# Q, K and V of the last two chunks as pairs of 64-row matmuls inside the gate-up stages

## The chip, the cores and the metric

The kernel runs on one core of one Trainium2 chip. The metric is device time in microseconds (us) of one execution, lower is better. The core's engines run side by side: TensorE (PE, with its weight loads PEld), VectorE (DVE), ScalarE (ACT), GpSimd (POOL) and SyncE (SP). SP and POOL issue nearly all DMAs here.

## The reference

One transformer block with modulation over S = 2048 tokens of D = 576 values, all bf16:

```
sa, ca, ga, sb, cb, gb = silu(c) @ w_mod            # six rows of 576
h = layernorm(x) * (1 + ca) + sa
q, k, v = h @ wqkv                                  # 32 heads of 18
attention: each token sees itself and the tokens 2, 4, .. 14 before it (8 logits, softmax)
x = x + ga * (attention @ wo)
h = layernorm(x) * (1 + cb) + sb
x = x + gb * (((h @ w_gate) * (h @ w_up)) @ w_down)  # width 4608
```

576 is four and a half times 128. A matmul that contracts over all 128 rows of the array needs five passes over 576, the last of them half empty. Two matmuls of 64 rows each can stand side by side in the array; 576 is nine times 64.

## The kernel before

**Chunks and groups.** Attention (the A part) works on eight chunks of 256 tokens. The feed-forward part works on five groups of 128-token tiles, `GROUPS = [(0, 2), (2, 6), (6, 10), (10, 13), (13, 16)]`: group 0 is chunk 0, group 1 chunks 1 and 2, group 2 chunks 3 and 4, group 3 chunk 5 and half of 6, group 4 the rest. Each group has a gate-up stage (`gate_up`, L651) and a down stage (`down`, L713). They alternate: gate-up 0, down 0, gate-up 1, down 1 and so on. The order of instructions on every engine is the order in which the program emits them (`manual_schedule`), and each engine works through its own in order.

**Gate-up.** It runs over 36 column tiles `f` of the width 4608. For each, the gate result goes to PSUM bank `pg` and the up result to `pu`. All its matmuls are 64 rows high and come in pairs: the lower half of the array works for one bank, the upper half for the other. `first_part` does five pairs (the 64 left-over rows, which `wgr` and `h2T` hold for both, then four), `second_part` does four pairs with the banks swapped. A wait (`swap`) stands ahead of the second part, so that both halves never write the same bank. The second part of tile f comes after the first part of tile f+1. Then ACT copies `pu` and `pg` to `u_sb` and `g_sb` (L683, L684), and DVE multiplies them into `hh` (L688). PSUM has eight banks, one pool (`ps`) for everything.

**Background of the gate-up stages.** Attention from the products of Q and K on: `b_p` (L424, DVE), logits `b_lq` (L434), softmax, weighting of shifted values and sums. `values(i)` issues `b_ld`, which loads the shifted values `vsh` of chunk i from a DRAM buffer `vd`. `B_two` orders two chunks, `B_one` one chunk. Each piece has a cost, and `spread` lays the list evenly over the column tiles.

**Down.** It runs over the 36 row tiles of w_down. Each of the group's token tiles gets a 512-column matmul into `acc` (L726) and a 64-column one into `accr` (L730). Its background, spread one piece after another over the first 32 steps, is made by `out_qkv(i, n)`: for chunk i the output projection (`b_o`, `b_w` L577), the second layer norm (`b_ln`, `b_norm`) and the transposes `b_t` that make `h2T`; and for chunk n the first layer norm (`a_ln`, `a_norm`), the transposes `a_t` that make `hT`, then five pieces `a_q` (L376) and two pieces `a_v` (L399, L401). A piece `a_q` does two column tiles of Q or of K with five 128-row matmuls each; the middle one does the left-over 64 columns of Q and of K together (`wq4`). ACT copies the results to `qT` and `kT`, and `a_halo` copies 16 earlier keys. `a_v` does one row tile of V as 504 and 72 columns; ACT copies to `v_sb`, and POOL stores that to `vd`. The rows 64 to 127 of the fifth row tile of `wqk`, `wv` and of the modulation columns `modc` are zero.

**Where chunks 5 to 8 stand.** Down 1 has `out_qkv(3, 5) + out_qkv(4, 6)` (32 pieces), down 2 has `out_qkv(5, 7) + out_qkv(6, 8)` (24 pieces; there is no chunk 8). The attention of chunk 6 is in gate-up 2, that of chunk 7 in gate-up 3.

**Weights.** `load_wgu` (L150, SP) and `load_wd` (L165, POOL) stream the gate, up and down weights in blocks of four tiles, into three buffers each.

Of the kernel before, what the change touches and what calls it, by code (L numbers as in the profile page):

```python
# [7 lines left out]
BF = mybir.dt.bfloat16  # L8
F32 = mybir.dt.float32
# [29 lines left out]

MODK = (0, 4, 1, 2, 3)  # L40
QKK = (0, 1, 4, 2, 3)
GROUPS = [(0, 2), (2, 6), (6, 10), (10, 13), (13, 16)]


@with_exitstack
def kernel(
# [47 lines left out]
    def js(j):  # L94
        return slice(j * P, (j + 1) * P)
# [5 lines left out]
    ind = consts.tile([P, KT, H], BF, name="ind")  # L101
    addc = consts.tile([P, 2, KT], F32, name="addc")
    eps = consts.tile([P, 1], F32, name="eps")
    modc = consts.tile([P, 4, KT], F32, name="modc")
    ga_bc = consts.tile([P, D], BF, name="ga_bc")
    gb_bc = consts.tile([P, D], BF, name="gb_bc")
    sc = consts.tile([P, KT], BF, name="sc")
# [175 lines left out]
    def modulate(dst, s, m, vi_scale, vi_shift, on_dve):  # L283
        if on_dve:
            nc.vector.tensor_scalar(dst, s, modc[:, vi_scale, m:m + 1], modc[:, vi_shift, m:m + 1], ALU.mult, ALU.add)  # L285
        else:
            nc.scalar.activation(dst, s, ACTF.Identity, bias=modc[:, vi_shift, m:m + 1], scale=modc[:, vi_scale, m:m + 1])

    def transposed(src, dst, cols, vi, between=None):
        n = P * len(cols)  # L290
        pA = ps([P, 3, n], BF, "tr_pA")
        pB = ps([P, 2, n], BF, "tr_pB")
        for c, j in enumerate(cols):
            if c and between:
                between()
            for m in range(KT):
                d = pA[:, m, :] if m < 3 else pB[:, m - 3, :]
                nc.tensor.transpose(d[:, js(c)], src[:, j, m * P:(m + 1) * P], ident[:])  # L298

        def evict(on_dve=(0, 1, 2)):  # L300
            for m in range(KT):
                s = pA[:, m, :] if m < 3 else pB[:, m - 3, :]
                modulate(dst(m), s, m, vi + 1, vi, m in on_dve)
        return evict

    def mod_columns(wm, pi):
# [50 lines left out]
    def a_t(i, on_dve=(0, 1, 2), between=None):  # L357
        a_tiles(i)
        hT = aa[i]["hT"]
        transposed(aa[i]["xn"], lambda m: hT[:, m, :], (0, 1), 0, between)(on_dve)  # L360

    def qk_w(kt, m):
        if m == KF:
# [30 lines left out]
    def a_v(i, j):  # L394
        hT = aa[i]["hT"]
        pv = ps([P, VA * DH], F32, "pv")
        pvr = ps([P, VR * DH], F32, "pvr")
        for kt in range(KT):
            nc.tensor.matmul(pv[:], lhsT=hT[:, kt, js(j)], rhs=wv[:, kt, 0:VA * DH], start=(kt == 0), stop=(kt == KT - 1))  # L399
        for kt in range(KT):  # L400
            nc.tensor.matmul(pvr[:], lhsT=hT[:, kt, js(j)], rhs=wv[:, kt, VA * DH:D], start=(kt == 0), stop=(kt == KT - 1))  # L401
# [95 lines left out]
    def b_o(i):  # L497
# [120 lines left out]
    def B_one(a, av_a):  # L618
        return B_pr(a, 0, 6) + B_lq(a, 0) + B_pr(a, 6, 8) + B_wait(1.5) + B_lq(a, 1) + B_wait(4.0) + B_sm(a) + av_a

    def B_av(i):
        r = []
# [6 lines left out]

    def out_qkv(i, n):  # L630
        o = [lambda: b_o(i), lambda: b_w(i, 0), lambda: b_w(i, 1), lambda: b_ln(i), lambda: b_norm(i), lambda: b_t(i, (0,) if i == 6 else (0, 1))]
        if n >= NCH:
            return [o[0], nop, o[1], o[2], o[3], o[4], nop, o[5]]
        q, v = [lambda g=g: a_q(n, g) for g in range(5)], [lambda j=j: a_v(n, j) for j in range(ST)]
        return ([lambda: a_ln(n), o[0], lambda: (a_norm(n), load_x(n + 2))] + [nop] * (3 if n == 4 else 0) + [o[1], lambda: a_t(n), o[2], o[3]] + q[:1] + [o[4]] + q[1:]
                + [o[5]] + v)
# [14 lines left out]
    def gate_up(gi, hh, bg):  # L651
        N = P * (GROUPS[gi][1] - GROUPS[gi][0])
        ht = h2T[gi]
        at = spread(bg, FT)
        lo, hi = slice(0, 64), slice(64, P)
        pgu = {}

        def half(bank, lhs, rhs, first, last):
            return nc.tensor.matmul(bank[:, 0:N], lhsT=lhs, rhs=rhs, start=first, stop=last, skip_group_check=True)  # L659

        def first_part(f):
            wb = wgu_blk[gi * NBLK + f // FB]
            cs = slice((f % FB) * P, (f % FB + 1) * P)
            pg, pu = ps([P, 2 * CH], F32, "pg"), ps([P, 2 * CH], F32, "pu")
            half(pg, wgr[lo, js(f)], ht[lo, KF, 0:N], True, False)
            half(pu, wgr[hi, js(f)], ht[hi, KF, 0:N], True, False)
            for k in range(KF):
                half(pg, wb[lo, k, 0, cs], ht[lo, k, 0:N], False, False)
                m = half(pu, wb[hi, k, 1, cs], ht[hi, k, 0:N], False, False)
            pgu[f] = (pg, pu, m)  # L670

        def second_part(f):
            wb = wgu_blk[gi * NBLK + f // FB]
            cs = slice((f % FB) * P, (f % FB + 1) * P)
            pg, pu, m = pgu.pop(f)
            swap = nc.tensor.nop()
            tc.add_manual_dep(swap.ins, m.ins.name, SYNC, reason="row tiles swap banks")
            for k in range(KF):
                half(pu, wb[lo, k, 1, cs], ht[lo, k, 0:N], False, k == KF - 1)
                half(pg, wb[hi, k, 0, cs], ht[hi, k, 0:N], False, k == KF - 1)  # L680
# [4 lines left out]
            return g, u  # L685

        def product(f, gu):
            nc.vector.tensor_tensor(hh[:, f, 0:N], gu[0][:, 0:N], gu[1][:, 0:N], ALU.mult)  # L688

        for f in range(FT):  # L690
            first_part(f)
            gu = second_part(f - 1) if f > 0 else None
            if f > 0 and f % FB == 0:
                ahead(gi, f // FB)
            for piece in at[f]:
                piece()
            if gu:
                product(f - 1, gu)
        product(FT - 1, second_part(FT - 1))
# [338 lines left out]
    def values(i):  # L1038
# [2 lines left out]
    gbg = {0: B_two(1, 2, B_av(1) + [res(2), (0.0, load_wm5), (0.0, lambda: load_wd(0))], []),  # L1041
           1: values(3) + B_two(3, 4, B_av(3) + [res(3), res(4)], B_av(4)),
           2: values(5) + B_two(5, 6, B_av(5) + [res(5), res(6)], B_av(6)),
           3: values(7) + B_one(7, B_av(7)) + [res(7)]}
    av2 = [p for _, p in B_av(2)]
    oq = out_qkv(1, 3)
    first = []
# [7 lines left out]
    def gb_row():  # L1055
# [3 lines left out]
        b_ld(2, 1)  # L1059
        load_wd(2)  # L1060

    dbg = {0: [gb_row] + first + out_qkv(2, 4),
           1: out_qkv(3, 5) + out_qkv(4, 6),
           2: out_qkv(5, 7) + out_qkv(6, 8),
           3: [nop, lambda: b_t(6, (1,))] + out_qkv(7, 8)}
    for gi in range(NG):
        if gi == 1:
            hh0_guard.__exit__(None, None, None)
            wgx_guard.__exit__(None, None, None)
            hhp = pool("hhp", 1)  # L1070
# [33 lines left out]
```

## Time and profile before

| | |
|---|---|
| time, median of 3 runs (lowest to highest) | 559.87 us (559.21 to 560.19) |
| time of the profiled execution | 560.52 us |
| its span | 558.7 us |
| TensorE matmuls | 547.8 us busy, 98% of the span |
| TensorE weight loads | 325.0 us, 58% |
| VectorE | 331.2 us, 59% |
| ScalarE | 250.6 us, 45% |
| GpSimd | 63.4 us, 11% |
| granted TensorE clock | full speed in every slice |
| DMA | 108.14 MB, mean 194 GB/s |
| last chain | PE 84%, DMA 10%, issue 3% |

The span is the time between the first and the last recorded work of the profiled execution; 1.8 us of its time lie around it. Matmuls are pipelined, so a matmul's recorded time is longer than what it costs in a row of matmuls; the distance from one start to the next is the cost.

### The profile page before, as it was taken

Reading aid. Unit: us, or ns where it says so; the run is one execution under the profiler, and the core shown is the slowest. Engines: PE = TensorE matmul, PEld = TensorE weight load, DVE = VectorE, ACT = ScalarE, POOL = GpSimd, SP = SyncE. Lnnn points to the kernel's source line nnn. Section 1 sums busy time; section 2 is a strip of 40 time slices with the busy share of each in tenths; the row PEclk is TensorE's granted clock in tenths of the full one; section 3 lists DMA queues with packets and bytes.
Section 4 is the critical chain, followed back from the end, with each engine's and each line's share of the span. In section 5 each row is a group of like instructions: output and inputs, shape, how many; then the busy total and the mean of one; then the engine's idle time right before and its main releaser. Section 6 shows DMA issues by size and latency. Waiting matters only on the chain.

```text
span 558.7 us, 14224 instructions
## 1 busy us (share of the span) xinstructions
PE 547.8 (98%) x5972; PEld 325.0 (58%) x6012; DVE 331.2 (59%) x796; ACT 250.6 (45%) x584; POOL 63.4 (11%) x97
## 2 busy tenths in 40 slices
PE   7999999999999999999999999999999999999997
PEld 4887796665444446656444445655565555555564
DVE  7888798984777776252858686406736614322202
ACT  2746666354465652323355654230466511456500
POOL 3103101123000001111100000111100022000020
PEclk9999999999999999999999999999999999999999
DMA  8999999645646745233834855234965565565053
GB/s 271 282 292 309 340 306 352 193 147 177 230 143 218 247 141 166 92 101 106 288 119 152 276 174 182 86 106 128 324 195 192 185 194 177 182 193 187 1 170 117
DMA packets 69994, 108.14 MB, mean 194 GB/s; under 512 B 3658, under 2 KB 57754, under 8 KB 69930
## 3 DMA queue, kind: packets, MB, share of 16 engines
q1 hardware_dynamic: 58672, 61.28, 35.2%
q0 software_dynamic: 11168, 45.81, 25.4%
q8 instruction: 47, 0.77, 0.6%
q14 instruction: 17, 0.14, 0.1%
q10 hardware_dynamic: 90, 0.15, 0.1%
HBM read 102.78 MB, written 4.44 MB: 192 GB/s over the span
## 4 chain that ended last, share of the span: by engine, by line
PE 84%; DMA 10%; issue 3%; SPq 1%; DVE 1%; POOL 0%; POOLq 0%
PE pg L659 26%; PE pu L659 21%; PE acc L726 20%; PE pq L376 4%; PE accr L730 4%; DMA wgr<-in_B_w_gate_dram 3%; PE pw L577 2%; PE pv L399 2%; DMA wo<-in_A_wo_dram 2%; DMA wgu<-in_B_w_up_dram 2%; DMA x_t<-in_A_x_dram 2%; PE lg L434 2%; DMA wd<-in_B_w_down_dram 1%; SPq L150 1%; DMA wmA<-in_w_mod_dram 1%
## 5 line engine op out<-in xcount | busy, mean ns | idle before, releaser
L659 PE MATMUL pg<-h2T,wgu 64*128 64x512 bf16 (+2 forms) x1440 | 277.3, 333 | 0.0
L659 PE MATMUL pu<-h2T,wgu 64*128 64x512 bf16 (+2 forms) x1440 | 275.8, 333 | 0.0
L659 PEld LDWEIGHTS <-wgu 64*128 64x128 bf16 x2880 | 142.8, 94 | 105.7 <-issue 0.5
L683 ACT CAST u_sb<-pu 128x512 bf16<-128x512 f32 (+2 forms) x180 | 90.2, 501 | 136.3 <-PE pg L659 134.7
L726 PE MATMUL acc<-wd,hh 128*128 128x512 bf16 (+1 forms) x554 | 140.2, 369 | 0.8 <-DMA wd<-in_B_w_down_dram 0.5
L688 DVE TENSOR_TENSOR hh<-g_sb,u_sb 128x512 bf16<-128x512 bf16 (+2 forms) x180 | 66.7, 372 | 99.3 <-ACT g_sb L684 97.8
L730 PE MATMUL accr<-wd,hh 128*128 128x64 bf16 x576 | 99.2, 193 | 1.6
L684 ACT CAST g_sb<-pg 128x512 bf16<-128x512 f32 (+2 forms) x180 | 91.3, 507 | 0.0
L726 PEld LDWEIGHTS <-hh 128*128 128x128 bf16 x588 | 55.3, 98 | 57.1 <-issue 1.7
L165 POOL DMA_DIRECT2D wd<-in_B_w_down_dram x45 | 33.9, 753 | 292.6 <-PE accr L730 270.5
L659 PE MATMUL pu<-h2T,wgr 64*128 64x512 bf16 (+2 forms) x180 | 60.2, 335 | 0.3 <-ACT u_sb L683 0.3
L659 PE MATMUL pg<-h2T,wgr 64*128 64x512 bf16 (+2 forms) x180 | 60.2, 335 | 0.2 <-DVE h2T L285 0.2
L730 PEld LDWEIGHTS <-hh 128*128 128x128 bf16 x576 | 51.7, 98 | 2.6 <-issue 0.7
L424 DVE TENSOR_TENSOR prod<-qT,kT 128x1280 bf16<-128x1280 bf16 x56 | 44.7, 818 | 2.5 <-PE lg L434 2.5
L484 DVE TENSOR_TENSOR vsh<-vsh,attn 128x1152 bf16<-128x1152 bf16 x56 | 41.0, 750 | 0.0
L285 DVE TENSOR_SCALAR h2T<-tr_pA,modc 128x256 bf16<-128x256 bf16 (+1 forms) x27 | 8.8, 382 | 36.8 <-PE tr_pA L298 36.8
L376 PE MATMUL pq<-hT,wqk 128*128 128x256 bf16 x240 | 30.0, 273 | 0.0
L376 PEld LDWEIGHTS <-wqk 128*128 128x128 bf16 x280 | 25.7, 98 | 4.8
L659 PEld LDWEIGHTS <-wgr 64*128 64x128 bf16 x360 | 18.1, 94 | 16.8 <-issue 4.5
L418 POOL DMA_DIRECT2D vsh<-vd x14 | 12.5, 892 | 123.3 <-DVE o_sb L495 84.4
L579 DVE TENSOR_TENSOR x<-pw,ga_bc 128x512 bf16<-128x512 f32 x14 | 9.7, 689 | 22.4 <-PE pw L577 22.1
L379 ACT CAST qT<-pq 128x512 bf16<-128x512 f32 x14 | 8.1, 581 | 28.3 <-PE pq L376 28.3
(196 smaller groups left out, 489.9 us busy)
## 6 DMA issues: line engine op xcount, KB each, us to landing
wd<-in_B_w_down_dram POOLq DMA_DIRECT2D x45, 576.0 KB, 4.4
wgu<-in_B_w_gate_dram SPq DMA_DIRECT2D x45, 512.0 KB, 4.0
wgu<-in_B_w_up_dram SPq DMA_DIRECT2D x45, 512.0 KB, 5.6
vsh<-vd POOLq DMA_DIRECT2D x14, 1152.0 KB, 8.9
x_r<-in_A_x_dram SPq DMA_DIRECT2D x8, 288.0 KB, 6.4
out_dram<-x SPq DMA_DIRECT2D x15, 144.0 KB, 5.4
x_t<-in_A_x_dram SPq DMA_DIRECT2D x7, 288.0 KB, 5.8
vd<-v_sb POOLq DMA_DIRECT2D x14, 144.0 KB, 3.1
```

The source lines that it names most:

```text
L165: return nc.gpsimd.dma_start(wb[:], B_w_down[r0:r0 + FB * P, :].rearrange("(k p) n -> p k n", p=P))
L376: nc.tensor.matmul(pq[:, gi, :], lhsT=qk_w(kt, m), rhs=hT[:, kt, cols], start=(kt == 0), stop=(kt == KT - 1))
L399: nc.tensor.matmul(pv[:], lhsT=hT[:, kt, js(j)], rhs=wv[:, kt, 0:VA * DH], start=(kt == 0), stop=(kt == KT - 1))
L418: return nc.gpsimd.dma_start(vsh[:].rearrange("p w d h -> p w (d h)"), vsrc)
L424: nc.vector.tensor_tensor(prod[:], aa[i]["qT"][:], aa[i]["kT"][:, :, off:off + CH], ALU.mult)
L484: nc.vector.tensor_tensor(v, v, at, ALU.mult)
L659: return nc.tensor.matmul(bank[:, 0:N], lhsT=lhs, rhs=rhs, start=first, stop=last, skip_group_check=True)
L683: nc.scalar.copy(u[:, 0:N], pu[:, 0:N])
L684: nc.scalar.copy(g[:, 0:N], pg[:, 0:N])
L688: nc.vector.tensor_tensor(hh[:, f, 0:N], gu[0][:, 0:N], gu[1][:, 0:N], ALU.mult)
L726: nc.tensor.matmul(a[:], lhsT=hh[:, f, js(j)], rhs=wb[:, f % FB, cs], start=(f == 0), stop=(f == FT - 1))
L730: nc.tensor.matmul(accr[:, j, :], lhsT=hh[:, f, js(j)], rhs=wb[:, f % FB, 512:D], start=(f == 0 and j == 0), stop=(f == FT - 1), skip_grou ...
```

## The change

`PAIRED = (6, 7)` names two chunks. For these `out_qkv` keeps the layer norm and the transposes `a_t` in the down stage, and leaves `a_q` and `a_v` out. In their place `qkv_units` makes five units a chunk, and `gate_up` runs them between its column tiles: a list `items` holds tiles and units, each with a first and a second part, and the second part of an item follows the first part of the next one. Chunk 6 has one unit after each of the column tiles 0 to 4 of gate-up 2. Chunk 7 has three units after tile 0 of gate-up 3, one after tile 1 and one after tile 2.

A unit computes two outputs into two banks `pp`, in nine pairs of 64-row matmuls per tile, with the banks swapped after the fifth. The units are: Q (column tiles 0 and 2, then 1 and 3, 256 wide), K (the same), the left-over 64 columns of Q and K (the chunk's two halves of 128 tokens), and V twice (two row tiles, 288 columns each).

The fifth row tile must then hold its 64 rows twice. `load_pair_rows`, one more piece at the end of down 0, loads these rows of `wqk` and `wv` again into partitions 64 to 127, copies those of `wq4`, and fills a sixth modulation column, which `a_t` of chunks 6 and 7 uses. For the other chunks `hT` stays zero there.

In gate-up 3 the background begins at tile 2 (`bg_from=2`), and `values(7)` moves from the list's head to behind four products of chunk 7. The rest of `gate_up` is rewritten into the item form, with the same order of instructions where there are no units.

```diff
+PAIRED = (6, 7)
-    modc = consts.tile([P, 4, KT], F32, name="modc")
+    modc = consts.tile([P, 4, KT + 1], F32, name="modc")
...
+    def load_pair_rows():
+        nc.sync.dma_start(wqk[64:, KF, :], A_wqkv[KF * P:D, 0:2 * D])
+        nc.sync.dma_start(wv[64:, KF, :], A_wqkv[KF * P:D, 2 * D:3 * D])
+        nc.gpsimd.tensor_copy(halves(wq4[64:, KF, :]), halves(wqk[64:, KF, :])[:, :, KF * P:D])
+        for r in (LO, HI):
+            nc.scalar.copy(modc[r, 0:2, KT], modc[0:64, 0:2, KF])
+
+    def pair_unit(width, tiles, evict):
+        st = {}
+
+        def first():
+            banks = [ps([P, len(tiles), width], F32, "pp") for _ in range(2)]
+            for t, ops in enumerate(tiles):
+                for k in (KF, 0, 1, 2, 3):
+                    for bank, rows, op in zip(banks, (LO, HI), ops):
+                        lhs, rhs = op(k)
+                        m = half(bank[:, t, :], lhs[rows], rhs[rows], t == 0 and k == KF, False)
+            st.update(banks=banks, m=m)
+
+        def second():
+            banks = st["banks"]
+            swap_after(st["m"])
+            for t, ops in enumerate(tiles):
+                for k in range(KF):
+                    for bank, rows, op in zip(banks[::-1], (LO, HI), ops[::-1]):
+                        lhs, rhs = op(k)
+                        half(bank[:, t, :], lhs[rows], rhs[rows], False, k == KF - 1)
+            evict(*banks)
+        return first, second
...
+        def qk4_out(a, b):
+            for j, t in enumerate((a, b)):
+                nc.scalar.copy(kT[0:64, KF, HALO + j * P:HALO + (j + 1) * P], t[64:P, 0, :])
+                nc.scalar.copy(qT[:, KF, js(j)], t[:, 0, :])
+            a_halo(i)
...
+        units = ([pair_unit(CH, [(qk_op(m), qk_op(m + 2)) for m in (0, 1)], q_out),
+                 pair_unit(CH, [(qk_op(m), qk_op(m + 2)) for m in (KT, KT + 1)], k_out),
+                 pair_unit(P, [(qk_op(KF, js(0)), qk_op(KF, js(1)))], qk4_out)]
+                + [pair_unit(288, [(v_op(0, hf), v_op(1, hf))], v_out(hf)) for hf in range(2)])
...
+    def B_one(a, ld, av_a):
+        return B_pr(a, 0, 4) + ld + B_pr(a, 4, 6) + B_lq(a, 0) + B_pr(a, 6, 8) + B_wait(1.5) + B_lq(a, 1) + B_wait(4.0) + B_sm(a) + av_a
...
+        if n in PAIRED:
+            return [lambda: a_ln(n), o[0], lambda: (a_norm(n), load_x(n + 2)), o[1], lambda: a_t(n), o[2], o[3], nop, o[4], nop, nop, o[5]]
...
+        items = []
         for f in range(FT):
+            items += [(lambda f=f: first_part(f), lambda f=f: second_part(f))] + units.get(f, [])
+        for k, (first, _) in enumerate(items):
+            first()
+            for piece in items[k - 1][1:] if k else at[0]:
                 piece()
+        items[-1][1]()
...
-           3: values(7) + B_one(7, B_av(7)) + [res(7)]}
+           3: B_one(7, values(7), B_av(7)) + [res(7)]}
...
+    dbg = {0: [gb_row] + first + out_qkv(2, 4) + [load_pair_rows],
...
+    units = {2: qkv_units(6, [(0, 0, 1), (1, 1, 2), (2, 2, 3), (3, 3, 4), (4, 4, 5)]),
+             3: qkv_units(7, [(0, 0, 3), (1, 3, 4), (2, 4, 5)])}
...
+        gate_up(gi, hh, gbg.get(gi, []), units.get(gi, {}), 2 if gi == 3 else 0)
```

More of the change, by code (lines that the diff above doesn't have):

```diff
@@ L287, in modulate, with transposed @@
             nc.scalar.activation(dst, s, ACTF.Identity, bias=modc[:, vi_shift, m:m + 1], scale=modc[:, vi_scale, m:m + 1])
-    def transposed(src, dst, cols, vi, between=None):
+    def transposed(src, dst, cols, vi, between=None, kf=KF):
         n = P * len(cols)
@@ L302, in evict @@
                 s = pA[:, m, :] if m < 3 else pB[:, m - 3, :]
-                modulate(dst(m), s, m, vi + 1, vi, m in on_dve)
+                modulate(dst(m), s, kf if m == KF else m, vi + 1, vi, m in on_dve)
         return evict
@@ L359, in a_t @@
         hT = aa[i]["hT"]
-        transposed(aa[i]["xn"], lambda m: hT[:, m, :], (0, 1), 0, between)(on_dve)
+        transposed(aa[i]["xn"], lambda m: hT[:, m, :], (0, 1), 0, between, KT if i in PAIRED else KF)(on_dve)
     def qk_w(kt, m):
@@ L507, in b_o, with half, swap_after @@
         nc.scalar.copy(oT[:, 4, :], pB[:, 0, :])
+    LO, HI = slice(0, 64), slice(64, P)
+    def half(dst, lhs, rhs, first, last):
+        return nc.tensor.matmul(dst, lhsT=lhs, rhs=rhs, start=first, stop=last, skip_group_check=True)
+    def swap_after(m):
+        swap = nc.tensor.nop()
+        tc.add_manual_dep(swap.ins, m.ins.name, SYNC, reason="row tiles swap banks")
+    def load_pair_rows():
[4 more added lines that the diff above has]
+            nc.scalar.copy(modc[r, 0:2, KT], modc[0:64, 0:2, KF])
@@ new lines, in qkv_units, with qk_op, v_op, q_out @@
+    def qkv_units(i, plan):
+        qT, kT = qTs[i % 2], kTs[i % 2]
+        vs = []
+        def qk_op(m, cols=slice(0, CH)):
+            return lambda k: (qk_w(k, m), aa[i]["hT"][:, k, cols])
+        def v_op(j, hf):
+            return lambda k: (aa[i]["hT"][:, k, js(j)], wv[:, k, 288 * hf:288 * (hf + 1)])
+        def q_out(a, b):
+            nc.scalar.copy(qT[:, 0:2, :], a[:])
+            nc.scalar.copy(qT[:, 2:4, :], b[:])
+        def k_out(a, b):
+            nc.scalar.copy(kT[:, 0:2, HALO:], a[:])
+            nc.scalar.copy(kT[:, 2:4, HALO:], b[:])
+        def qk4_out(a, b):
[3 more added lines that the diff above has]
+            a_halo(i)
+        def v_out(hf):
+            def out_(a, b):
+                for j, t in enumerate((a, b)):
+                    if hf == 0:
+                        vs.append(vstage.tile([P, DH, H], BF, name="v_sb"))
+                    nc.scalar.copy(vs[j][:, :, 16 * hf:16 * (hf + 1)], t[:, 0, :].rearrange("p (h d) -> p d h", d=DH))
+                    if hf == 1:
+                        r0 = HALO + i * CH + j * P
+                        nc.gpsimd.dma_start(vd[r0:r0 + P, :], vs[j][:].rearrange("p d h -> p (d h)"))
+            return out_
+        units = ([pair_unit(CH, [(qk_op(m), qk_op(m + 2)) for m in (0, 1)], q_out),
+                 pair_unit(CH, [(qk_op(m), qk_op(m + 2)) for m in (KT, KT + 1)], k_out),
+                 pair_unit(P, [(qk_op(KF, js(0)), qk_op(KF, js(1)))], qk4_out)]
+                + [pair_unit(288, [(v_op(0, hf), v_op(1, hf))], v_out(hf)) for hf in range(2)])
+        return {f: units[a:b] for f, a, b in plan}
@@ L616, in B_two @@
                 + B_pr(b, 6, 8) + av_a[:4] + B_lq(b, 1) + av_a[4:] + B_sm(b) + av_b)
-    def B_one(a, av_a):
-        return B_pr(a, 0, 6) + B_lq(a, 0) + B_pr(a, 6, 8) + B_wait(1.5) + B_lq(a, 1) + B_wait(4.0) + B_sm(a) + av_a
+    def B_one(a, ld, av_a):
+        return B_pr(a, 0, 4) + ld + B_pr(a, 4, 6) + B_lq(a, 0) + B_pr(a, 6, 8) + B_wait(1.5) + B_lq(a, 1) + B_wait(4.0) + B_sm(a) + av_a
     def B_av(i):
@@ L631, in out_qkv @@
         o = [lambda: b_o(i), lambda: b_w(i, 0), lambda: b_w(i, 1), lambda: b_ln(i), lambda: b_norm(i), lambda: b_t(i, (0,) if i == 6 else (0, 1))]
-        if n >= NCH:
+        if n >= NCH or n == 5 and n in PAIRED:
             return [o[0], nop, o[1], o[2], o[3], o[4], nop, o[5]]
+        if n in PAIRED:
+            return [lambda: a_ln(n), o[0], lambda: (a_norm(n), load_x(n + 2)), o[1], lambda: a_t(n), o[2], o[3], nop, o[4], nop, nop, o[5]]
         q, v = [lambda g=g: a_q(n, g) for g in range(5)], [lambda j=j: a_v(n, j) for j in range(ST)]
@@ L648, in spread, with gate_up @@
         return at
-    def gate_up(gi, hh, bg):
+    def gate_up(gi, hh, bg, units={}, bg_from=0):
         N = P * (GROUPS[gi][1] - GROUPS[gi][0])
         ht = h2T[gi]
-        at = spread(bg, FT)
-        lo, hi = slice(0, 64), slice(64, P)
+        at = [[] for _ in range(bg_from)] + spread(bg, FT - bg_from) + [[]]
         pgu = {}
-        def half(bank, lhs, rhs, first, last):
-            return nc.tensor.matmul(bank[:, 0:N], lhsT=lhs, rhs=rhs, start=first, stop=last, skip_group_check=True)
         def first_part(f):
@@ L664, in first_part @@
             pg, pu = ps([P, 2 * CH], F32, "pg"), ps([P, 2 * CH], F32, "pu")
-            half(pg, wgr[lo, js(f)], ht[lo, KF, 0:N], True, False)
-            half(pu, wgr[hi, js(f)], ht[hi, KF, 0:N], True, False)
+            half(pg[:, 0:N], wgr[LO, js(f)], ht[LO, KF, 0:N], True, False)
+            half(pu[:, 0:N], wgr[HI, js(f)], ht[HI, KF, 0:N], True, False)
             for k in range(KF):
-                half(pg, wb[lo, k, 0, cs], ht[lo, k, 0:N], False, False)
-                m = half(pu, wb[hi, k, 1, cs], ht[hi, k, 0:N], False, False)
+                half(pg[:, 0:N], wb[LO, k, 0, cs], ht[LO, k, 0:N], False, False)
+                m = half(pu[:, 0:N], wb[HI, k, 1, cs], ht[HI, k, 0:N], False, False)
             pgu[f] = (pg, pu, m)
@@ L675, in second_part @@
             pg, pu, m = pgu.pop(f)
-            swap = nc.tensor.nop()
-            tc.add_manual_dep(swap.ins, m.ins.name, SYNC, reason="row tiles swap banks")
+            swap_after(m)
             for k in range(KF):
-                half(pu, wb[lo, k, 1, cs], ht[lo, k, 0:N], False, k == KF - 1)
-                half(pg, wb[hi, k, 0, cs], ht[hi, k, 0:N], False, k == KF - 1)
+                half(pu[:, 0:N], wb[LO, k, 1, cs], ht[LO, k, 0:N], False, k == KF - 1)
+                half(pg[:, 0:N], wb[HI, k, 0, cs], ht[HI, k, 0:N], False, k == KF - 1)
             g = gup.tile([P, 2 * CH], BF, name="g_sb")
@@ L684, in second_part @@
             nc.scalar.copy(g[:, 0:N], pg[:, 0:N])
-            return g, u
-        def product(f, gu):
-            nc.vector.tensor_tensor(hh[:, f, 0:N], gu[0][:, 0:N], gu[1][:, 0:N], ALU.mult)
-        for f in range(FT):
[L691 to L695, printed above, removed]
+            if f < FT - 1 and f % FB == FB - 1:
+                ahead(gi, f // FB + 1)
+            for piece in at[f + 1]:
+                piece()
+            nc.vector.tensor_tensor(hh[:, f, 0:N], g[:, 0:N], u[:, 0:N], ALU.mult)
+        items = []
+        for f in range(FT):
+            items += [(lambda f=f: first_part(f), lambda f=f: second_part(f))] + units.get(f, [])
+        for k, (first, _) in enumerate(items):
+            first()
+            for piece in items[k - 1][1:] if k else at[0]:
                 piece()
-            if gu:
-                product(f - 1, gu)
-        product(FT - 1, second_part(FT - 1))
+        items[-1][1]()
         ahead(gi, NBLK)
@@ L1060, in gb_row @@
         load_wd(2)
-    dbg = {0: [gb_row] + first + out_qkv(2, 4),
+    dbg = {0: [gb_row] + first + out_qkv(2, 4) + [load_pair_rows],
            1: out_qkv(3, 5) + out_qkv(4, 6),
@@ L1071 @@
         hh = hhp.tile([P, FT, 2 * CH], BF, name="hh") if gi else hh0
-        gate_up(gi, hh, gbg.get(gi, []))
+        gate_up(gi, hh, gbg.get(gi, []), units.get(gi, {}), 2 if gi == 3 else 0)
         down(gi, hh, dbg.get(gi, []))
```

## The prediction

> **What bounds the kernel now.** I read the page first (busy shares, chain), then who TensorE waits for, then the PE timeline where the moved work runs, and last the stages around it.
>
> ```profile
> PE 547.8 (98%) x5972; PEld 325.0 (58%) x6012; DVE 331.2 (59%) x796; ACT 250.6 (45%) x584; POOL 63.4 (11%) x97
> ```
>
> ```profile
> PE idle L192 <- DVE hT L187: 1.3, 1, 1.3
> ...
> PE tr_pA L298 <- DVE ln_xn L263: 0.5, 2, 0.4
> PE acc L726 <- DMA wd<-in_B_w_down_dram: 0.5, 1, 0.5
> ```
>
> The second view is TensorE's list of waits (total us, times, longest). No entry of it falls after 205 us: from the down stage of group 1 on TensorE waits for nobody. The stages concerned, cut at their first matmuls, are down 1, gate-up 2, down 2, gate-up 3, with the columns span, PE, PEld, DVE, ACT, POOL (counts in brackets), clock, DMA share, GB/s:
>
> ```profile
> 207.39:266.05 58.66, 58.13 (x511) 35.56 (x522) 25.07 (x70) 18.89 (x47) 8.24 (x12) 1.00 0.37 115
> 266.05:339.90 73.85, 73.85 (x737) 33.22 (x738) 56.11 (x113) 40.36 (x76) 4.28 (x5) 1.00 0.61 203
> 339.90:390.15 50.25, 49.78 (x431) 28.91 (x439) 20.86 (x57) 12.72 (x32) 7.16 (x10) 1.00 0.40 122
> 390.15:444.90 54.75, 54.75 (x693) 33.81 (x692) 33.34 (x78) 31.28 (x73) 2.52 (x3) 1.00 0.68 224
> ```
>
> In all four the PE column is the span, at a granted clock of 1.00. So time moves one for one with TensorE's start-to-start time, and with new waits. A busy time is no price (pipelined matmuls overlap); the distance between starts is.
>
> **Removed.** For one chunk (here chunk 6, in down 1), each piece priced from its start to the start of what follows:
>
> ```profile
> 246.20 1.26 PE L376 MATMUL pq<-hT,wqk 128*128 128x256 bf16 x10
> 247.29 0.38 PE L726 MATMUL acc<-wd,hh 128*128 128x512 bf16 x1
> ...
> 251.32 0.71 PE L376 MATMUL pq<-hT,wq 128*128 128x256 bf16 x5
> 251.87 0.38 PE L726 MATMUL acc<-wd,hh 128*128 128x512 bf16 x1
> ...
> 258.53 1.23 PE L399 MATMUL pv<-wv,hT 128*128 128x504 bf16 x5
> 259.60 0.33 PE L401 MATMUL pvr<-wv,hT 128*128 128x72 bf16 x5
> 259.75 0.38 PE L726 MATMUL acc<-wd,hh 128*128 128x512 bf16 x1
> ```
>
> Four Q/K pieces of ten: 4 x 1.09 = 4.36. The piece of five (the 64 left-over columns of Q and of K): 0.55. V, two row tiles: 2 x 1.22 = 2.44. Sum 7.35 us a chunk, 14.70 us for two. It is all on the path.
>
> **Added.** A unit computes two outputs over 576 rows as nine slots; a slot is a lower-half and an upper-half matmul side by side. The gate-up stages already do this, and the distance between first matmuls of such slots prices it:
>
> ```profile
> 49.73 0.27 PE L659 MATMUL pg<-h2T,wgr 64*128 64x256 bf16 x1 [0.20 <-DVE h2T L285]
> ...
> 50.27 0.27 PE L659 MATMUL pg<-h2T,wgr 64*128 64x256 bf16 x1
> ```
>
> ```profile
> 390.98 0.32 PE L659 MATMUL pg<-h2T,wgr 64*128 64x384 bf16 x1
> ...
> 392.44 0.32 PE L659 MATMUL pg<-h2T,wgr 64*128 64x384 bf16 x1
> ```
>
> The first distance holds five slots of 256 columns: 0.54/5 = 0.109 us a slot. The second holds nine of 384 columns: 1.46/9 = 0.162. Per chunk:
> - Q and K, two units of two column tiles each: 36 slots of 256: 36 x 0.109 = 3.92 us.
> - V, two units of 288 columns: between the two slots above, 0.109 + 32/128 x 0.053 = 0.122; 18 x 0.122 = 2.20 us.
> - The left-over tile, one unit of 128 columns: no paired slot of that width is in the trace. Full-height transposes of 128 columns start 0.056 apart (241.33, 241.50 after three): a lower bound if halves overlap fully. Two such one after the other give 0.111, the upper bound. Which end? It hangs on two weight loads a slot. Sixteen 64-column matmuls in a row, each with a load of its own, take 0.47 us, 0.029 each:
>
> ```profile
> 262.12 0.47 PE accr L730 x16
> ```
>
> Two loads then take 0.058, and I take that: 9 x 0.058 = 0.52 us (bounds 0.50 and 1.00).
>
> Sum 6.64 us a chunk, 13.28 for two (bounds 13.2 and 14.2). Net 14.70 - 13.28 = **-1.4 us** (-1.5 to -0.5): a tenth of the slots saved (9 for 10), no more.
>
> A page rule speaks against this. The Trainium skill, "TensorE: Matmul & The Clock Gate", section "LDWEIGHTS (loading the stationary operand)", says that a load costs its columns over 1.2 per ns, whatever its rows; by it two loads a slot take 213 ns (an estimate from that page), the 126 slots 26.8 us, and the kernel would be 12 us slower. This trace contradicts it: nine-slot stages with two loads a slot run at 0.109, and full loads at 0.029. It is kept as a rival of its own below.
>
> **What moves with it.** *Down stages.* Lists 1 and 2 of background pieces shrink from 32 to 28 and from 24 to 20, spread over the same 32 steps of about 0.98 us, without the matmuls that lay between. What could be late is the last chain: the second `b_w`, layer norm, transposes of `b_t`. In down 2 now it takes 4.8 us, from pw's end at 381.0 to the transposes at 385.86, over five steps, with no wait worth the name. In both lists it gets seven steps, 6.9 us. If it came short, the transposes would wait on ln_xn. *The end of gate-up 2's input:* `b_t(4)` moves to step 31; 16 x 0.245 = 3.9 us of matmuls follow, and its evictions need about 1.4 (3 x 0.4 on DVE, 2 x 0.55 on ACT).
>
> *ACT.* Chunk 7's burst is the densest: three units after the first column tile. Per chunk ACT adds 4 x 0.586 (Q, K), 4 x 0.264 and the halo copy 0.261 (left-over), 4 x 0.40 (V, between 0.226 for 72 and 0.581 for 504 columns): 5.3 us. With 3 x 0.96 for u_sb and g_sb that is 8.2 us in 11.0 us of TensorE, from gate-up 3's start to the third column tile's end. PSUM has eight banks, two per item. Walked through in order: f0's second half ends at 2.56 and its banks are free at 3.7; Q's second half at 4.5, free at 5.9, wanted by V at 6.7; K's free at 7.1, wanted at 8.0; the left-over unit's free at 8.2, wanted at 9.3. The first units take banks that DVE frees from acc within 0.8 us. Smallest margin 0.8 us: no wait.
>
> *DVE.* Chunk 7's products wait for its halo copy, now 8.4 us into gate-up 3; `bg_from=2` puts them there, and only the gate-up product of tile 1 stands behind the first, itself not ready before 9.4. *Queues.* The two vd stores of V leave the down stages on POOL, where they stood between wd loads, and the vsh loads of chunk 7 start some 16 us later, beside a wgu load due two blocks (11.7 us) after issue; the slowest wgu load of that stage landed in 11.2 beside those same vsh loads, so the cover is thin but equal. The vsh rows are used 20 us after. The three one-off steps at down 0's end (two small SP loads, a POOL copy near 0.3 us, two ACT copies) precede work with a whole gate-up stage of 70 us to spare. On SP only output stores stand behind them, on POOL a wd load and chunk 3's vsh loads.
>
> **Rivals.**
> 1. *The narrow unit is bound by its loads* (or paired slots with changing operands cost some ns more). Upper bound 1.00 for 0.52, twice: net -0.45, time 559.4. For: no such row in the trace. Against: 0.029 a load.
> 2. *Evictions gate the units (slower).* At the start of gate-up 2 and 3, ten units each wait for a bank until ACT has emptied it. Each would lose what an eviction pair (1.17 plus about 0.2 latency) exceeds its cover, a neighbour's half of some 0.9: 0.45; ten times 0.45 = 4.5, net +3.1, time 563.0. It decides from 0.14 us a unit. For: ACT at three quarters in that stretch. Against: margins of 0.8 us.
> 3. *The two halves of a unit do not overlap*, each waiting for its own load. Slots then cost twice: 36 x 0.218 + 18 x 0.244 + 9 x 0.111 = 13.2 a chunk; net 2 x (13.2 - 7.35) = +11.8, time 571.7. The 0.109 slots speak against it. (The skill's load rule above would act like this.)
> 4. *A little more than the slots is saved*, such as tight background chains relaxed: about -2, time 557.9. For it speaks only that the transposes came just behind ln_xn.
>
> **The numbers.** The profiled execution took 560.52 us with a span of 558.70; the median of the three runs is 559.87, and the same difference is taken off it: 559.87 - 1.4 = 558.5. Chances: forecast 0.62 (its own range 558.0 to 559.1), rival 1 0.18, rival 2 0.14, rival 3 0.02, rival 4 0.04. Forecast and rival 1 hold 0.80; with a run-to-run scatter of about 0.4 around them the range is 557.9 to 559.9. About 0.2% (1.1 us, 558.75) is what a measurement of this kernel can tell from no change; the forecast clears it by 0.3 only. Faster: four fifths of the forecast and rival 4, 0.54. Same: the rest of the forecast and rival 1, 0.30. Slower: 0.16.
>
> **What would show it.** Down 1 should shrink from 58.7 to 51.3 and down 2 from 50.3 to 42.9; gate-up 2 should grow from 73.9 to 80.5 and gate-up 3 from 54.8 to 61.4, PE full in each. Unit slots should start 0.109, 0.122 and 0.058 apart; 0.11 at 128 columns is rival 1. Waits of pp, pg or pu on ACT above 0.1 us each are rival 2. A down stage that shrinks by less, with transposes waiting on ln_xn, would break my cover there.

## The result, and the profile after

The changed kernel takes 558.58 us (median of 22 runs, 558.05 to 560.60), the kernel before 559.84 us beside it (22 runs, 558.93 to 560.82). The ratio of the runs is 0.9982, 95% interval 0.9976 to 0.9989. The change is faster, by about as much as the prediction called measurable (0.2%). The profiled execution took 558.37 us with a span of 556.5 us.

The busy shares of the changed kernel, from its page:

```profile
PE 548.4 (99%) x6134; PEld 323.8 (58%) x6134; DVE 331.1 (60%) x796; ACT 251.1 (45%) x590; POOL 63.1 (11%) x98
```

By the weight loads the kernel has 122 matmuls more than before (6012 to 6134), as the code of the two kernels has it. The trace of the kernel before has only 5972 matmul records beside its 6012 loads, so 40 are missing there, and the two busy times, 547.8 and 548.4, can't be compared. The stages can, since they are measured between starts. Down 1, gate-up 2, down 2 and gate-up 3 of the changed kernel, cut at their first matmuls, with the same columns as before the change:

```profile
206.78:258.07 51.29, 51.29 (x457) 29.86 (x455) 24.92 (x70) 14.39 (x36) 7.14 (x10) 1.00 0.42 125
258.07:338.57 80.50, 80.50 (x864) 38.97 (x863) 56.14 (x113) 45.05 (x89) 5.42 (x7) 1.00 0.58 190
338.57:381.51 42.94, 42.94 (x375) 23.25 (x374) 20.53 (x57) 8.22 (x21) 6.00 (x8) 1.00 0.44 136
381.51:442.87 61.36, 61.36 (x819) 38.00 (x819) 33.67 (x78) 35.98 (x86) 3.66 (x5) 1.00 0.63 205
```

The PE column equals the span in all four. Together they take 236.09 us; in the kernel before, cut at the first matmuls of its timeline, they take 58.66, 73.86, 50.31 and 54.76, together 237.59 (the prediction's cuts lie up to 0.07 later, with a sum of 237.51). That is -1.50 us. The rest of the difference of the two spans lies elsewhere, and most of it is scatter: the stretch ahead of gate-up 0, where both kernels run the same code at a DMA share of 1.03, took 49.73 us before and 49.05 here. Over all profiles of this study it took between 48.73 and 50.58, while a later stage repeats within about 0.05 us. So I read the effect of each edit from stage lengths, and the medians only say whether the sum arrives.

The first units of chunk 6 on TensorE (timeline of the changed kernel: start, us, engine, line, operation, tiles, shape, count):

```profile
259.16 1.25 PE L513 MATMUL pp<-hT,wqk 64*128 64x256 bf16 x20
260.25 0.38 PE L513 MATMUL pu<-h2T,wgu 64*128 64x512 bf16 x1
...
262.19 2.13 PE L513 MATMUL pp<-hT,wqk 64*128 64x256 bf16 x36
264.15 0.38 PE L513 MATMUL pu<-h2T,wgu 64*128 64x512 bf16 x1
...
266.10 1.03 PE L513 MATMUL pp<-hT,wqk 64*128 64x256 bf16 x16
266.97 0.44 PE L513 MATMUL pp<-hT,wq 64*128 64x128 bf16 x10
267.25 0.38 PE L513 MATMUL pu<-h2T,wgu 64*128 64x512 bf16 x1
...
269.19 0.39 PE L513 MATMUL pp<-hT,wq 64*128 64x128 bf16 x8
269.42 0.78 PE L513 MATMUL pp<-wv,hT 64*128 64x288 bf16 x10
270.03 0.38 PE L513 MATMUL pu<-h2T,wgu 64*128 64x512 bf16 x1
```

Two matmuls are one slot. From start to start: 10 slots of 256 columns in 1.09 us, 18 in 1.96 and 8 in 0.87 (0.109 each), 9 narrow slots in 0.28 + 0.23 (0.057 each), 5 slots of V in 0.61 (0.122 each). Nothing waits between them: TensorE's list of waits, asked for the four stages alone (206.78 to 442.87), is empty, and `pp` is in no entry of the whole list.

ScalarE's share in the burst (groups of the changed kernel between 258 and 285 us, with the mean ns of one behind the comma):

```profile
L578 ACT CAST v_sb<-pp 128x288 bf16<-128x288 f32 x4 | 1.4, 402 | 1.8 <-PE pp L513 1.8
L570 ACT CAST qT<-pp 128x128 bf16<-128x128 f32 x2 | 0.5, 265 | 0.0
L569 ACT CAST kT<-pp 64x128 bf16<-64x128 f32 x2 | 0.5, 262 | 0.3 <-PE pp L513 0.2
```

These were costed at 0.40 and 0.264. The releasers at the end of the rows say that ACT waited for TensorE, never the other way.

### The profile page after: what moved, and what is told of

Read it like the earlier page. It is cut to its first block, busy times and chain, and to the rows that moved or that the text cites. A ratio compares the mean times of both kernels' runs of the same rounds, so it can differ in the third digit from the quotient of the medians.

```text
span 556.5 us, 14517 instructions
## 1 busy us (share of the span) xinstructions
PE 548.4 (99%) x6134; PEld 323.8 (58%) x6134; DVE 331.1 (60%) x796; ACT 251.1 (45%) x590; POOL 63.1 (11%) x98
## 4 chain that ended last, share of the span: by engine, by line
PE 84%; DMA 8%; DVE 6%; ACT 1%; issue 1%; SPq 0%; ACTq 0%
PE pg L513 28%; PE pu L513 22%; PE acc L803 20%; DMA wgr<-in_B_w_gate_dram 3%; PE accr L807 3%; PE pp L513 2%; PE pw L658 2%; DMA wo<-in_A_wo_dram 2%; PE pq L377 2%; PE lg L435 2%; DMA wgu<-in_B_w_gate_dram 1%; DMA x_t<-in_A_x_dram 1%; DVE vsh L485 1%; PE pv L400 1%; DMA wmA<-in_w_mod_dram 1%; DVE ln_xn L264 1%
## 5 line engine op out<-in xcount | busy, mean ns | idle before, releaser
L803 PE MATMUL acc<-wd,hh 128*128 128x512 bf16 (+1 forms) x588 | 143.7, 370 | 0.1
L660 DVE TENSOR_TENSOR x<-pw,ga_bc 128x512 bf16<-128x512 f32 x14 | 9.6, 688 | 20.9 <-PE pw L658 20.9
L492 DVE TENSOR_TENSOR vsh<-vsh 128x1152 bf16<-128x1152 bf16 x28 | 20.6, 753 | 0.0
L377 PEld LDWEIGHTS <-wqk 128*128 128x128 bf16 x200 | 18.3, 98 | 3.2
L377 PE MATMUL pq<-hT,wqk 128*128 128x256 bf16 x160 | 20.1, 273 | 0.0
```

The costliest lines, as they stand in the source:

```text
L377: nc.tensor.matmul(pq[:, gi, :], lhsT=qk_w(kt, m), rhs=hT[:, kt, cols], start=(kt == 0), stop=(kt == KT - 1))
L492: nc.vector.tensor_tensor(vsh[:, d], vsh[:, d], vsh[:, 4 + 2 * s:6 + 2 * s], ALU.add)
L803: nc.tensor.matmul(a[:], lhsT=hh[:, f, js(j)], rhs=wb[:, f % FB, cs], start=(f == 0), stop=(f == FT - 1))
```

## The experiments

My theory: time follows TensorE's slots (nine for ten), the place of the work matters only through what stands beside it, and nothing new waits. Rivals: the gain comes from moving the work out of the down stages whatever its form; or from pairing whatever the place; or from something else that the change touches. Stage lengths are in the order down 1, gate-up 2, down 2, gate-up 3, and "four stages" is their sum against 237.59.

**The same place, with 128-row matmuls.** Units stay where the change has them, but compute each output with five full-height passes.

```diff
 def pair_unit(width, tiles, evict):
+    def one(bank, which):
+        for t, ops in enumerate(tiles):
+            for k in range(KT):
+                lhs, rhs = ops[which](k)
+                nc.tensor.matmul(bank[:, t, :], lhsT=lhs, rhs=rhs, start=(k == 0), stop=(k == KT - 1))
     def first():   # now: one(bank 0, first output)
     def second():  # now: one(bank 1, second output), then evict
-dbg = {0: [gb_row] + first + out_qkv(2, 4) + [load_pair_rows],
+dbg = {0: [gb_row] + first + out_qkv(2, 4),
```

> Q, K and V of chunks 6 and 7 stand where the change puts them, but as 128-row matmuls, ten passes for two outputs in place of nine paired slots (first part: five passes for the first output; second part: five for the second). Theory (only the number of slots counts): what leaves the down stages, 7.35 us a chunk, comes back in full in the gate-up stages, so nothing is gained; on top, the array now changes between 64-row and 128-row work inside the gate-up stages. At a stage border of the profile this costs about 0.10 us (matmul of 512 columns at 257.75, next start at 258.07, 0.216 of it streaming). Six runs of units in gate-up 2 and five in gate-up 3 make 22 borders: +2.2 us, about 562.0. Rival (the gain comes from relieving the down stages, pairing is incidental): about 558.5, as with the change. Rival (moving is free and borders cost nothing): 559.8.

Measured: 562.19 us (561.40 to 562.98), ratio 1.0042, interval 1.0029 to 1.0056. Stages 51.28, 82.52, 42.94, 63.16; four stages +2.31. Moving alone loses. Start of the first unit's first half in gate-up 2 (timeline of this kernel):

```profile
258.02 0.38 PE L513 MATMUL pg<-h2T,wgu 64*128 64x512 bf16 x1
...
258.33 1.27 PE L533 MATMUL pp<-hT,wqk 128*128 128x256 bf16 x10
259.53 0.39 PE L513 MATMUL pu<-h2T,wgu 64*128 64x512 bf16 x1
```

A gate-up matmul is followed after 0.21 us by the next one of its half; here the full-height one starts after 0.31, and its ten matmuls, 1.09 in the down stage, take 1.20. About 0.10 us goes at each border between 64-row and 128-row matmuls. The stages say the same: gate-up 2 has 12 borders more than before, (82.52 - 73.86 - 7.35)/12 = 0.109; gate-up 3 has 10, (63.16 - 54.76 - 7.35)/10 = 0.105. The Trainium skill, "TensorEngine Tiling (Array Packing)", section "Key Properties", states that a change of the tiling mode drains TensorE. It gives no price. The 0.1 us at each border here agrees with it.

**The same pairs, left in the down stages.**

```diff
-return [lambda: a_ln(n), o[0], ..., o[2], o[3], nop, o[4], nop, nop, o[5]]
+u = [lambda k=k: (us[k][0][0](), us[k][0][1]()) for k in range(5)]   # first and second half in one piece
+return [lambda: a_ln(n), o[0], ..., o[2], o[3], u[0], o[4], u[1], nop, u[2], nop, o[5], u[3], u[4]]
...
-units = {2: qkv_units(6, ...), 3: qkv_units(7, ...)}
+units = {}   # values(7) first again, background of gate-up 3 from tile 0
```

> The same ten paired units, but left in the down stages, each as one background piece with its second part right behind its first. Theory: the slots save 1.4 us, but each unit has two borders between 128-row and 64-row work (0.10 each, 2.0 us in all) and its swap waits for its own last matmul to drain with nothing in between (recorded 0.269 less the slot 0.109 = 0.16, with the semaphore about 0.2, 2.0 us in all): net about +2.6, 562.4; the down stages should be 7.35 - 6.64 - 0.2*10/2*... that is about 1.3 us longer each, gate-up unchanged at 73.9 and 54.8. Rival (pairing alone counts, wherever it stands): 558.5.

Measured: 563.88 us, ratio 1.0077, interval 1.0064 to 1.0090. Stages 60.36, 73.86, 52.02, 54.72; four stages +3.37. Pairing alone loses more. One unit in down 1 (timeline of this kernel):

```profile
247.15 0.19 PE L809 MATMUL accr<-wd,hh 128*128 128x64 bf16 x1
247.28 2.38 PE L513 MATMUL pp<-hT,wqk 64*128 64x256 bf16 x36
249.59 0.39 PE L805 MATMUL acc<-wd,hh 128*128 128x512 bf16 x1
```

The 18 slots that cost 1.96 us in gate-up 2 take 2.31 here, and another 0.10 goes ahead of them (accr to the next start is 0.13, elsewhere in this stretch 0.03). By the stages, down 1 is 60.36 - 51.29 = 9.07 longer than without this work, for 6.64 us of slots: 0.49 a unit, where I had expected 0.4. Two borders are 0.21 of it. The rest, 0.25 to 0.28, is the swap: with both halves in one piece nothing stands between the last matmul of the first half and the first one of the second, which must wait for it. The weight loads of the same unit show that wait:

```profile
247.27 0.99 PEld L513 LDWEIGHTS <-wqk 64*128 64x128 bf16 x20 [0.24 <-issue]
248.60 0.77 PEld L513 LDWEIGHTS <-wqk 64*128 64x128 bf16 x16 [0.34 <-PE pp L513]
```

The ten slots of the first half cost 1.09 us in gate-up 2; here the second half's loads start 1.33 after the first half's, 0.24 later, released by the last `pp` matmul. In the gate-up stages the neighbour's half fills that gap. So neither place nor form alone brings the gain; the pair needs neighbours of its own height, and another item to put between its halves.

**One chunk, three chunks.** First chunk 6 alone is paired, then chunks 5, 6 and 7. For the latter the transposed chunk 5 lies in a `vsh` buffer, and gate-up 2 runs ten units.

```diff
-PAIRED = (6, 7)
+PAIRED = (6,)          # units of chunk 7 and bg_from taken out
...
-PAIRED = (6, 7)
+PAIRED = (5, 6, 7)
+units[2]: qkv_units(5, [(0, 0, 3), (1, 3, 4), (2, 4, 5)]) and qkv_units(6, [(3, 0, 1), (4, 1, 2), (5, 2, 3), (6, 3, 4), (7, 4, 5)])
+values(5) behind the first four products of chunk 5, bg_from 2 in gate-up 2 as well
```

> Only chunk 6 is paired; chunk 7 keeps its 128-row matmuls in down 2, and gate-up 3 its old background order. Theory (each chunk saves 7.35 - 6.64 = 0.7 us of slots, no waits, no fixed cost): down 1 51.3, gate-up 2 80.5, down 2 50.3, gate-up 3 54.8; half of the change, about 559.1. Rival (a fixed cost of the one-off row loads, or a wait in one of the two stages that the other outweighs): down 1 and gate-up 2 together not 0.7 below 132.5, time 559.8 or 558.5.

> Chunk 5 is paired as well: its units stand after tiles 0 to 2 of gate-up 2, those of chunk 6 after tiles 3 to 7, and gate-up 2's background starts at tile 2 with the loads of chunk 5's values behind four products. Theory (0.7 us a chunk adds up, evictions keep their margins): down 1 about 44.0, gate-up 2 about 87.1, in all -2.1 us against the kernel before, about 557.7. Rival (evictions on ACT or the attention work on DVE gate the denser gate-up 2): waits of pp, pg or pu on ACT, or of lg on DVE, of more than 0.7 us together, and no time below that of the change, 558.5 or more.

Measured: chunk 6 alone 559.87 us, ratio 1.0003 (0.9991 to 1.0015), stages 51.29, 80.50, 50.31, 54.72, four stages -0.77. Three chunks 559.10 us, ratio 0.9983 (0.9974 to 0.9992), stages 43.93, 87.14, 42.94, 61.37, four stages -2.21. Two of the windows of the kernel with three:

```profile
207.50:251.43 43.93, 43.51 (x382) 24.14 (x389) 24.97 (x70) 9.86 (x25) 6.06 (x8) 1.00 0.45 139
251.43:338.57 87.14, 87.14 (x989) 44.63 (x989) 56.49 (x113) 49.81 (x102) 6.56 (x9) 1.00 0.55 179
```

By the stages each chunk brings 0.71 to 0.77 us, three times in a row (-0.77, -1.50, -2.21), as expected, and even ten units in one stage wait for nothing: PE is full over 87.14 us. But the medians don't follow. One chunk, forecast at 559.1, shows no gain, and three, forecast at 557.7, show no more than two. Something outside the four stages must eat it, or come and go between executions.

**The preparation without the pairs, and the two kernels again.** `load_pair_rows` stays at the end of down 0, but nothing is paired; beside it the change and the three-chunk kernel once more.

```diff
-PAIRED = (6, 7)
+PAIRED = ()
-units = {2: qkv_units(6, ...), 3: qkv_units(7, ...)}
+units = {}
```

> The change without its units: no chunk is paired, Q, K and V of all chunks stay 128-row matmuls in the down stages, but the one-off row loads at the end of down 0, the sixth modulation column and the rewritten loop are there. Theory 1 (these cost nothing; what the three-chunk and the one-chunk kernel lacked in whole time against their stage lengths, 1.4 and 0.7 us, is scatter of the part ahead of gate-up 0): stages 58.7, 73.9, 50.3, 54.8 as in the kernel before, gate-up 0 starting at 49 to 50, time 559.8. Theory 2 (the one-off steps or the shifted tile addresses slow the start for good): gate-up 0 starts, or down 0 ends, 0.5 to 1 us later in most runs, time 560.4 to 560.8.

> The change itself, on the same chip as the other two. From its stage lengths (down 1, gate-up 2, down 2, gate-up 3: 1.50 us less in sum than before): 558.3. Theory 2 would leave it at 558.9 or more.

> Chunks 5, 6 and 7 paired, on the same chip as the change. Its stages sum to 2.2 us less than before, 0.67 less than the change. Theory 1: 557.6, and faster than the change in the same call by about 0.7. Theory 2 (its start is later for good): no faster than the change, 558.5 to 559.1, with gate-up 0 starting 0.7 to 1.4 later than in the change.

Measured beside a kernel before of 560.17: preparation alone 560.61 us, ratio 1.0010 (1.0000 to 1.0021), four stages -0.03; the change 558.57, ratio 0.9975 (0.9966 to 0.9985), stages 51.29, 80.50, 42.95, 61.36; three chunks 559.18, ratio 0.9988 (0.9972 to 1.0004), runs from 557.67 to 563.40. The preparation seems to cost some tenths, though the interval reaches zero. Neither theory for the three chunks holds: they are no faster than the change, but in the one profile of each gate-up 0 doesn't start later either (49.51, in the change 49.94). And the profile of the three-chunk kernel caught an execution in which gate-up 3 took 63.45 instead of 61.37. TensorE's waits of that execution, and the line on landing for `wgu` between 378 and 446 us:

```profile
PE pu L513 <- DMA wgu<-in_B_w_up_dram: 1.0, 1, 1.0
PE pg L513 <- DMA wgu<-in_B_w_gate_dram: 0.8, 2, 0.6
```

```profile
DMA to landing us min/median/max: 3.6/4.7/12.4
```

The two `vsh` loads of chunk 7 were issued at 398.24, the gate and up weights of a block from 400.64 on, and one of these needed 12.4 us where two blocks of TensorE's work are 11.7. The change has the same loads in the same order; its slowest landing was 8.9 us in one profile and 9.1 in the other, and the kernel before had 11.2. That the row loads make the weights late is a guess from this order so far.

**The second row load held back.** The second `vsh` load of chunk 7 goes behind a later weight block; once on top of the change, once on top of three chunks.

```diff
-return B_pr(a, 0, 4) + ld + ... + B_lq(a, 1) + B_wait(4.0) + ...
+return B_pr(a, 0, 4) + ld[:1] + ... + B_lq(a, 1) + ld[1:] + B_wait(4.0) + ...
-3: B_one(7, values(7), B_av(7)) + [res(7)]}
+3: B_one(7, [(0.0, lambda: b_ld(7, 0)), (0.0, lambda: behind(b_ld(7, 1), wgu_in[3 * NBLK + 4]))], B_av(7)) + [res(7)]}
```

> The change, with the second load of chunk 7's values (1152 KB) held back until the fifth block of gate and up weights of gate-up 3 has landed, so that the two value loads no longer run together beside a weight load. In the repeat of the three-chunk kernel they did: a weight block took 12.4 us to land, against some 11.7 us of cover, and TensorE lost 2.1 us in gate-up 3. Theory (that collision, and not the units, costs time in some executions): the slowest weight load of gate-up 3 lands in 8 us or less (8.9 and 9.1 in the two profiles of the change), gate-up 3 is 61.4, the time 558.3 and its upper tail is shorter; never slower than the change. Rival (the loads have nothing to do with the spread): landing 9 us or more, or the same upper tail as the change (559.3 to 560.6).

> Chunks 5, 6 and 7 paired, with the same held-back load. Theory: gate-up 3 is 61.4 in the profile, no wait of TensorE on weights there, the time about 558.0 to 558.4 (stage sum 557.7 plus the later start seen in two medians of 559.1 to 559.2), so ahead of the three-chunk kernel without it by 0.7 or more. Rival (the start ahead of gate-up 0 accounts for all that it lacks): 559.1 again.

Measured beside 559.70: on the change 558.86 us (557.80 to 559.83), ratio 0.9982 (0.9973 to 0.9992); on three chunks 557.93 us (557.21 to 558.59), ratio 0.9968 (0.9956 to 0.9980). The four stages are unchanged by it, -1.50 and -2.21. Landing of `wgu` in gate-up 3 of the first:

```profile
DMA to landing us min/median/max: 3.6/4.4/5.8
```

The slowest landing fell from about 9 to 5.8 us, as meant, but the change's median and its spread did not improve: there the late landing was no regular cost, and I had expected 558.3 and a shorter tail. With three chunks the median fell by more than the 0.7 expected, from 559.10 and 559.18 to 557.93, and six runs spread over 1.4 us; without the edit eleven runs of that kernel had spread over 1.7 and twelve others over 5.7. But the slowest landing was still 9.9 us, TensorE did not wait for it, and the stages are those of the first three-chunk profile, so the profiles don't show where the median's fall comes from. That the edit removes the late landings for good, or that the row loads cause them, isn't shown: a landing that TensorE waits for was caught in one profile alone.

**Down 0, where the preparation stands.** In nine profiles of kernels with `load_pair_rows` as a piece of its own, down 0 took 43.91 to 43.96 us, once 43.70. Without it (first experiment) it took 43.32, and 43.79 in the kernel before, whose profile has a wait of 0.5 for `wd` there. The loads run on other engines' queues, but the piece is the 51st of a list that is spread evenly over 32 steps. So I hung it on the last of 50 pieces.

```diff
-dbg = {0: [gb_row] + first + out_qkv(2, 4) + [load_pair_rows],
+oq4 = out_qkv(2, 4)
+dbg = {0: [gb_row] + first + oq4[:-1] + [lambda: (oq4[-1](), load_pair_rows())],
```

> The change with one thing different: the loads of the fixed row halves are hung on the last piece of down 0's list, which so keeps the 50 pieces that it has in the kernel before, instead of being a piece of their own, the 51st. Theory: the 51st piece spreads the list of down 0 anew, so that transposes there meet their inputs a step too early and TensorE stands still for 0.3 to 0.6 us. Then down 0 takes 43.3 us (43.8 if the first down weights are late by 0.5, as in the kernel before) instead of 43.9, the four stages of the change stay 51.3, 80.5, 42.9 and 61.4, and the median falls by 0.3 to 0.6 from the change's 558.6, to about 558.1. Rival: the row loads themselves cost the time, or the stage ahead of gate-up 0 does; then down 0 stays at 43.9 and the median at 558.6.

> The kernel with chunks 5, 6 and 7 in gate-up stages and the second rearranged row load held back, and its fixed row loads hung on the last of 50 pieces of down 0's list, as in the run beside it. Theory: down 0 takes 43.3 us instead of 43.9, the four later stages stay 43.9, 87.1, 42.9 and 61.4, and the median is 557.4, 0.3 to 0.6 below the 557.9 of the same kernel with 51 pieces. Rival: down 0 stays at 43.9, and the median at 557.9.

Measured beside 560.16: on the change 558.43 us (557.62 to 559.27; I had expected 558.1), ratio 0.9968 (0.9956 to 0.9980), down 0 43.62 with a wait of 0.3 for `wd` in it; on three chunks with the load held back 557.29 us (557.07 to 557.69), ratio 0.9951 (0.9939 to 0.9964), down 0 43.32. Down 0 of the change, and below it that of the second kernel, in both without a wait for `wd`:

```profile
89.00:132.92 43.92, 43.32 (x387) 26.97 (x386) 35.24 (x92) 20.59 (x55) 9.25 (x14) 1.00 0.61 190
```

```profile
89.41:132.73 43.32, 42.97 (x387) 26.98 (x386) 35.01 (x92) 20.62 (x55) 9.26 (x14) 1.00 0.64 205
```

The same number of matmuls, 0.60 us less. Where it went is in the timelines of the weight loads (PEld) and of TensorE: first the change, at the transposes of `b_t(1)`, then the second kernel, at the same transposes.

```profile
108.93 0.31 PEld L299 LDWEIGHTS <-ln_xn 128*128 128x128 bf16 x5 [0.29 <-DVE ln_xn L264]
109.48 0.31 PEld L299 LDWEIGHTS <-ln_xn 128*128 128x128 bf16 x5 [0.24 <-DVE ln_xn L264]
```

```profile
109.62 0.57 PEld L299 LDWEIGHTS <-ln_xn 128*128 128x128 bf16 x10
```

And the second `b_w` of chunk 2, in the change and in the second kernel:

```profile
117.99 0.31 PE L658 MATMUL pwr<-wo,oT 128*128 128x64 bf16 x5
118.44 1.24 PE L658 MATMUL pw<-wo,oT 128*128 128x512 bf16 x5
```

```profile
118.58 0.31 PE L658 MATMUL pwr<-wo,oT 128*128 128x64 bf16 x5
118.73 1.24 PE L658 MATMUL pw<-wo,oT 128*128 128x512 bf16 x5
```

With 51 pieces some fall a step earlier. The transposes meet a normalized tile that isn't ready: on TensorE they start 0.18 us late, and the second five start 0.55 after the first instead of 0.28. And `pw` follows `pwr` after 0.45 instead of 0.15; the chain of the change has it released by VectorE's work on the first `pw` (L660), which ends at 118.39. That is 0.18 + 0.27 + 0.30 = 0.75 us lost. A gap of 0.15 comes off, which the second kernel has and the change hasn't: at the next transposes (117.38) its second five start after 0.43 instead of 0.28. The balance is 0.60, as measured. In executions with a late `wd` ahead of these places less is to be had: the list of 51 stays between 43.70 and 43.96 with waits for `wd` of 0.2 to 0.4, which fits late inputs that get their time by it, while the list of 50 goes to 43.62 with 0.3 and 43.79 with 0.5. So by what the profiles caught the piece costs 0.60 us where `wd` is in time, about 0.3 where it is late by 0.3 (43.93 and 43.96 beside 43.62), and nothing that can be seen where it is late by 0.4 or 0.5 (43.70 beside 43.79). The medians with three chunks are in line with it (557.93 to 557.29, in two batches of runs whose intervals overlap); on top of the change, 558.43 can't be told from 558.58.

## Why the prediction was right, and where it was off

- **Removed: right.** 14.70 us forecast; the down stages lost 58.66 - 51.29 = 7.37 and 50.31 - 42.94 = 7.37, together 14.74.
- **Added: right.** 13.28 forecast; the gate-up stages gained 6.64 and 6.60, together 13.24. The slots cost 0.109 and 0.122 as taken. The narrow slot, the one price with no row of its own, was put at 0.058 and measured 0.057. The upper bound (0.111) is out. Whether two loads (0.058) or the streaming of 128 columns (0.056) sets the slot's time isn't shown, since 0.057 lies between them. What spoke against the change was the reading that loads add up one after another on the path, and that reading fails by the same rows: two loads a slot fit into 0.057 us, though the trace records 0.094 for each of them, so they overlap. The duration that the Trainium skill gives for such a load ("TensorE: Matmul & The Clock Gate", section "LDWEIGHTS (loading the stationary operand)"), its columns over 1.2 in ns, is 0.107 us here (an estimate from that page). It is near the recorded 0.094 and is no price on the path.
- **No new waits on ACT or DVE: right.** None in the four stages; the experiment with ten units in gate-up 2 shows that a stage has room for twice as many.
- **The down stages' last chains: right.** Both shrank by the full amount; no transposes waited for `ln_xn` there.
- **The rivals.** Load-bound narrow units and unpaired halves fall with the slot distances, gated units with the empty list of waits. "A little more than the slots" is not seen: the four stages moved by -1.50 against a forecast of -1.42.
- **A misreading that did no harm.** The prediction says that the PE column is the span in all four stages. In the two down stages it is 58.13 of 58.66 and 49.78 of 50.25. Nine of the 144 records of `acc` are missing in each; the stage lengths and prices go from start to start, so the sum doesn't change.
- **Missed: "The three one-off steps at down 0's end ... precede work with a whole gate-up stage of 70 us to spare."** True of their data, but the step costs a place in the list. The 51st piece respread the 50 others and cost 0.60 us against a list of 50 where `wd` is in time; against the profile of before, with its own wait for `wd`, it is 0.13. This is a term of up to 0.6 that the sum lacked. The medians, which moved by 1.26 and in the second measurement by 1.60, fit a gain of 1.5 less a few tenths, and can't place it more closely.
- **Weak: "the cover is thin but equal".** Equal to the kernel before it was, and in the change no profile shows a wait for `wgu` in gate-up 3. But in the three-chunk kernel, which has this part alike, one execution lost 2.1 us to it. The prediction named the margin (11.2 of 11.7 us) and gave it no price.
- **The time and the chances.** 558.5 forecast, 558.58 measured. The forecast stood 0.3 us beyond what a measurement can tell from no change, and the result stands 0.2 beyond it: as close as the prediction had put it. That the median came within 0.1 us of the forecast is in part luck: with the same slot prices the medians of one and of three chunks missed theirs by 0.8 and 1.4, and the sum had no term for down 0. Why one chunk showed no gain at all stays open. The stage lengths are what bears the mechanism out.

The best version of this study pairs three chunks, holds the second row load back and hangs the preparation on an existing piece: 557.29 us, ratio 0.9951 (0.9939 to 0.9964). It beats both kernels: its slowest run, 557.69, is below the fastest of the change, 558.05.

## What to carry to other kernels

Cost a moved matmul by the distance between starts of its kind in the stage that receives it, and add the borders: here half-height pairs paid only among other half-height work, with something between their two halves. Where background work is spread evenly over a loop, a new piece that gives the busy engine no work still moves all the others; hang it on one that is there, or look again at the whole list. When the start of a kernel is bound by DMA and scatters more than the edit is worth, compare stage lengths, and use the median only as a check on their sum.

## What the runs showed of the hardware

Each border between 64-row and 128-row matmuls costs 0.10 to 0.11 us on TensorE, and a swap of halves between two banks with nothing in between about 0.25. A slot of two 64-row matmuls of 128 columns, each with a weight load of its own, runs at 0.057 us. The stretch at the head of the kernel, with a DMA share of 1.03, varies by 1.9 us between executions of the same code. The slowest weight load of gate-up 3 took 8.9 to 11.2 us in nine profiles without the held-back row load and 12.4 in a tenth; in the three with it, 5.8, 9.9 and 6.8.
